# Two layers of linear attention and MLP on one core: one tile transposed before it is scaled, one chunk divided by token, and the queues in a new order

## The chip, the cores and the metric

The kernel runs on one core of a Trainium2 chip. A core has five engines that run their own instruction queues: TensorE (PE in the profile; its weight loads are PEld), VectorE (DVE), ScalarE (ACT), GpSimd (POOL) and SyncE (SP, which here only issues DMAs). They wait for each other with semaphores. The metric is the device time of one execution in microseconds, lower is better.

## The reference

The input is x with 2048 tokens of 512 features. Two layers follow; each is attention and then an MLP, with the same weights in both layers.

```python
def _layernorm(x, axis=-1, eps=1e-5):
    m = jnp.mean(x, axis=axis, keepdims=True)
    v = jnp.var(x, axis=axis, keepdims=True)
    return (x - m) / jnp.sqrt(v + eps)

def _A_ref(x, wqkv, wo):            # 32 heads of 16
    q, k, v = qkv[0], qkv[1], qkv[2]
    phi = lambda t: jnp.where(t > 0, t + 1, jnp.exp(t)) + 1e-6
    pq, pk = phi(q), phi(k)
    kv = jnp.einsum("bhsd,bhse->bhde", pk, v)
    z = jnp.einsum("bhsd->bhd", pk)
    num = jnp.einsum("bhqd,bhde->bhqe", pq, kv)
    den = jnp.einsum("bhqd,bhd->bhq", pq, z)[..., None] + 1e-6
    o = num / den
    ...
def _B_ref(x, w1, b1, w2, b2):
    y = _layernorm(x, axis=-1)
    h = _gelu(jnp.einsum("bsd,df->bsf", y, w1) + b1)
    return jnp.einsum("bsf,fd->bsd", h, w2) + b2

x = x + _A_ref(_layernorm(x, axis=-1), A_wqkv, A_wo)
x = x + _B_ref(_layernorm(x, axis=-1), B_w1, B_b1, B_w2, B_b2)
... # and both lines once more
```

Since kv and z are sums over all tokens, no token's attention output can be formed before every key of the layer is known.

## The kernel before

**Tiles.** The 2048 tokens are 16 tiles of 128 rows, in four chunks of four tiles. The code counts layers, chunks and tiles from zero; an operation's name holds the layer, the tile (or the chunk and a number in it), and sometimes a part: `K0_3` is the key projection of tile 3 in layer 0, `Q0_1_2` the query projection of part 2 of chunk 1, `W10_0_13_1` the up projection of layer 0, chunk 0, column block 13, second half of the chunk. The titles' "layer one" is layer 0 in the code, the "second chunk" is chunk 1, and "tile one" is tile 0.

**One layer.** For each tile: `stats` and `aggr` (DVE, lines 773 and 775) give mean and variance, `veps` (DVE or POOL, 780) adds epsilon, `pow` (POOL, 782) gives the reciprocal root, and `norm` writes the normalised tile y in bf16 (DVE 795, or ACT 790 with POOL's `nmr`). Tile 3 of layer 0 has its sums made by ACT (`sum`, `neg`, `sq`, lines 764 to 770). y is transposed, either by PE through an identity into PSUM (`PTA`, 817) and copied out by ACT (`tc`, 827), or by a DMA transpose that SP issues (`TA`, 804). In layer 0 tiles 0 to 5 go by PE, the other ten by DMA. Then come `K` (four matmuls, 866) and `phi` (834 to 856: ACT `exp` and mostly ACT `relu`, DVE `min`, and a sum on DVE or POOL), and `G`, which sums y transposed times phi(k) over all tiles (958 in layer 0), `Z` (941), which sums phi(k), and `Q` (883 by token, 896 by feature) with its own phi.

**The end of an attention block.** `KV` (1008) times the values' weights, masked per head, and `M` (1031) times the output weights fold all of the keys and values into one 512 x 512 matrix. `WO` (1097) multiplies a tile of phi(q), divided by its denominator, by that matrix; `RA` (DVE, 1102) adds the residual and sets the bank of PSUM free.

**The denominator** (`attn_den`, 1035 on) has two forms, and the table `WAY` says which chunk takes which. By feature: per chunk four `D` matmuls (1074) against a masked z, ACT `ln` (1076) and `rec` (exp of minus it, 1078), and a product `pr` (1082). By token: `pz` (a product of phi(q) with z's row, 1051, POOL or DVE), `red` (a sum per head, DVE, 1054), `den` (adds 1e-6, 1057), `rec` (DVE, 1059), `pr` (1063, POOL or DVE), and then `TP`, a DMA transpose that SP issues (1067). z's row is `zrow`, which PE's `ZR` (1022) and ACT's `cpz0` (971) make. Before, chunks 0 and 1 of layer 0 and chunk 0 of layer 1 go by feature, the others by token.

**The MLP.** A second normalisation (`statsB`, `powB`, `normB`, `TB`), the up projection `W1` (1127), ACT's gelu (1132), the down projection `W2` (1163) and `RB`. `b2` (1113) adds the bias to the residual. In the last layer `OD` stores each tile. The last tile of all, 15, is computed in two halves of columns, h0 and h1, with an addition (1155) and a store (1157) of its own for each.

**The order.** Each engine's queue is written out in `CONF["ORDER"]`, a list of names for each of the five. `CONF["PLACES"]` says which operation uses which buffer and bank after which other, and `CONF["WAY"]` which engine does an operation that more than one can do. A program works out the semaphore waits from this. An engine never passes an operation that waits.

**The start.** PE first runs `warm0` and `warm1`, together fifteen matmuls of 512 columns on constants (747), and then `PTA0_0`, `PTA0_1`, `K0_0`. The loads of x, of the key weights `wk` and the query weights `wq` are issued by SP and ACT; the bias loads `b1` and `b2` by SP among the transposes (`b2` between `TA0_12` and `TA0_10`), `Tb1` transposes b1, and ACT's `b1c` copies it. The weights `wv`, `wo`, `w1`, `w2` are loaded by POOL, after all of layer 0's transposes.

## Time and profile before

| what | us |
|---|---|
| median of three runs | 328.95 (328.55 to 329.53) |
| the profiled execution | 327.5 |
| its span, first to last instruction | 326.3 |
| ACT busy, POOL busy in it | 193.1, 152.5 |
| busy time of DVE, and its share of the span | 211.0, 65% |
| the last matmul group starts at | 322.44 |

The span is the time from the first to the last instruction of one execution that was recorded by the profiler. Busy times are for each engine alone, and the engines work side by side, so they do not add up to the span. A line that is 1% of the span is 3.3 us. The duration of a matmul in the records includes its way through the array: groups of matmuls follow each other sooner than their durations say, and the chain of waits shows the times from start to start.

In the tables, "<-" in a group's name stands between what an instruction writes and what it reads; "idle before" is the time in which the engine stood still ahead of that group, with the name of what it waited for.

### The profile page before, as it was taken

The page shows a single profiled execution, that of the slowest core. Times are in us where ns is not written, and L with a number is a line of the kernel's source. Part 1 is how long each engine was busy: PE and PEld are TensorE (multiplying, and loading weights), DVE is VectorE, ACT ScalarE, POOL GpSimd, SP SyncE. Part 2 cuts the span into 40 slices and gives each one's busy share as a digit, 9 for nine tenths or more (in the row PEclk, how much of TensorE's full clock was granted, in tenths as well). Part 3 has the DMA queues.
Part 4 walks back from the last instruction along what each step waited for, and adds up shares of the span by engine and source line. Part 5 has one row for each costly group of instructions (what it writes and reads, how often), then busy time and mean ns, then how long its engine had stood idle before and what let it go on. Part 6 is the DMA issues. An engine that isn't in the chain of part 4 may idle for free.

```text
span 326.3 us, 4763 instructions
## 1 busy us (share of the span) xinstructions
PE 322.2 (99%) x1723; PEld 159.3 (49%) x1723; DVE 211.0 (65%) x503; ACT 193.1 (59%) x334; POOL 152.5 (47%) x224
## 2 busy tenths in 40 slices
PE   8999999999999999999999999999999999999997
PEld 3444445576454444444444444458644444444444
DVE  5987679996938685142436899999989983300112
ACT  4988769797661416529673477969833454551600
POOL 5662548588663417300757434783856593100000
PEclk9999999999999999999999999999999999999999
DMA  7355753334012210331011110012034322200102
GB/s 266 120 83 97 219 189 104 105 64 68 16 32 50 54 26 3 80 64 34 0 32 33 34 32 0 19 32 50 17 82 94 69 48 66 64 0 2 64 0 80
DMA packets 46883, 20.37 MB, mean 62 GB/s; under 512 B 41932, under 2 KB 45388, under 8 KB 46860
## 3 DMA queue, kind: packets, MB, share of 16 engines
q1 hardware_dynamic: 44572, 13.00, 18.8%
q0 software_dynamic: 1056, 4.72, 4.5%
q10 hardware_dynamic: 1232, 2.36, 2.0%
q8 instruction: 13, 0.21, 0.3%
q14 instruction: 10, 0.08, 0.1%
HBM read 8.00 MB, written 2.10 MB: 31 GB/s over the span
## 4 chain that ended last, share of the span: by engine, by line
PE 97%; DVE 1%; ACT 1%; issue 0%
PE ps L1127 30%; PE ps L1163 29%; PE ps L1097 9%; PE ps L866 8%; PE ps L883 5%; PE ps L987 4%; PE ps L958 4%; PE ps L896 2%; PE ps L747 2%; PE ps L1150 1%; PE ps L1074 1%; PE ps L1008 1%; PE ps L1031 1%; PE ps L941 1%; PE ps L817 0%; DVE pkb L854 0%
## 5 line engine op out<-in xcount | busy, mean ns | idle before, releaser
L1132 ACT ACTIVATE gT<-ps,b1c 128x512 bf16<-128x512 f32 (+1 forms) x140 | 77.1, 600 | 65.3 <-PE ps L1127 65.0
L1127 PE MATMUL ps<-t,w 128*128 128x512 bf16 (+1 forms) x560 | 102.2, 336 | 0.0
L1163 PE MATMUL ps<-w,gT 128*128 128x512 bf16 x434 | 97.6, 379 | 0.0
L1127 PEld LDWEIGHTS ps<-t,w 128*128 128x128 bf16 x560 | 54.6, 98 | 43.7 <-ACT t L827 0.3
L1163 PEld LDWEIGHTS ps<-w,gT 128*128 128x128 bf16 x434 | 42.5, 98 | 50.4 <-DVE xsb L1169 0.2
L782 POOL TENSOR_TENSOR rstd<-veps,neghalf 128x1 f32<-128x1 f32 x64 | 37.9, 602 | 33.5 <-DVE veps L780 31.4
L837 ACT ACTIVATE eb<-ps 128x512 bf16<-128x512 f32 x64 | 37.4, 614 | 18.3 <-PE ps L866 10.5
L1173 DVE TENSOR_TENSOR outb<-ps,xsb 128x512 bf16<-128x512 f32 x15 | 10.1, 686 | 46.3 <-PE ps L1163 40.3
L773 DVE BATCH_NORM_STATS2 stats<-xsb 128x6 f32<-128x512 f32 x48 | 32.3, 678 | 0.4
L848 ACT ACTIVATE rb<-ps 128x512 bf16<-128x512 f32 x45 | 26.6, 617 | 9.2 <-PE ps L866 8.7
L866 PE MATMUL ps<-wqkv,t 128*128 128x512 bf16 x128 | 31.6, 379 | 0.1
L1097 PE MATMUL ps<-gtb,t 128*128 128x512 bf16 x128 | 31.2, 379 | 0.1
L850 DVE TENSOR_SCALAR eb<-eb 128x512 bf16<-128x512 bf16 x45 | 14.0, 321 | 21.1 <-ACT eb L837 21.1
L1113 POOL TENSOR_TENSOR xsb<-xsb,b2b 128x512 f32<-128x512 f32 x20 | 24.3, 1224 | 6.8 <-ACT yb L790 6.6
L790 ACT ACTIVATE yb<-xsb,nmr,rstd 128x512 bf16<-128x512 f32 x21 | 16.7, 812 | 14.2 <-POOL nmr L787 13.9
L780 POOL TENSOR_SCALAR veps<-mv 128x1 f32<-128x1 f32 x35 | 7.6, 217 | 30.8 <-DVE mv L775 28.1
L1063 POOL TENSOR_TENSOR t<-t,rr 128x512 bf16<-128x512 bf16 x14 | 15.5, 1114 | 13.6 <-DVE rr L1059 12.9
L795 DVE TENSOR_SCALAR yb<-xsb,mv,rstd 128x512 bf16<-128x512 f32 x27 | 16.1, 602 | 8.5 <-POOL rstd L782 8.3
L1051 POOL TENSOR_TENSOR lr<-t,zrow 128x512 f32<-128x512 bf16 x15 | 17.9, 1191 | 5.7 <-ACT zrow L971 4.2
L883 PE MATMUL ps<-wqkv,t 128*128 128x512 bf16 x80 | 19.9, 379 | 0.0
L1097 PEld LDWEIGHTS ps<-gtb,t 128*128 128x128 bf16 x128 | 12.3, 98 | 14.7 <-DVE rr L1059 0.6
L866 PEld LDWEIGHTS ps<-wqkv,t 128*128 128x128 bf16 x128 | 12.0, 98 | 14.9 <-ACT t L827 1.0
(97 smaller groups left out, 373.5 us busy)
## 6 DMA issues: line engine op xcount, KB each, us to landing
w<-in_B_w_dram POOLq DMA_DIRECT2D x4, 896.0 KB, 6.9
out_dram<-outb SPq DMA_DIRECT2D x15, 128.0 KB, 1.9
t<-in_A_x_dram ACTq DMA_DIRECT2D x3, 512.0 KB, 4.6
t<-yb SPq DMA_TRANSPOSE x56, 2.5
wqkv<-in_A_wqkv_dram ACTq DMA_DIRECT2D x1, 512.0 KB, 5.8
wqkv<-in_A_wqkv_dram POOLq DMA_DIRECT2D x1, 512.0 KB, 4.6
wo<-in_A_wo_dram POOLq DMA_DIRECT2D x1, 512.0 KB, 5.5
t<-in_A_x_dram SPq DMA_DIRECT2D x1, 384.0 KB, 3.1
```

The costliest lines, as they stand in the source:

```text
L773: G.op("dve", lambda e: e.bn_stats(stats[:, s.slot, :], src()), 620, reads=src_keys, writes=[k + "s"], tiles=[s, *src_tiles], name=f"stats ...
L782: G.op("pool", lambda e: e.tensor_tensor(rstd[:, s.slot:s.slot + 1], veps[:, s.slot:s.slot + 1], neghalf[:], op=ALU.pow), 570, reads=[k + ...
L837: G.op("act", lambda e: e.activation(eb[:, et.slot, :], bank(bt), ACT.Exp), 478, reads=[src_key], writes=[f"e{tag}"], tiles=[bt, et], name ...
L848: G.op("act", lambda e: e.activation(rb[:, rt.slot, :], bank(bt), ACT.Relu), 478, reads=[src_key], writes=[f"r{tag}"], tiles=[bt, rt], nam ...
L866: ins = e.matmul(bank(b), lhsT=yTa(yT)[:, dt, k * P:(k + 1) * P], rhs=wqkv[:, dt, D:2 * D], start=(dt == 0), stop=(dt == DT - 1))
L883: ins = e.matmul(bank(b), lhsT=yTa(yT)[:, dt, k * P:(k + 1) * P], rhs=wqkv[:, dt, 0:D], start=(dt == 0), stop=(dt == DT - 1))
L1051: lambda e, r=r, tok=tok: e.tensor_tensor(lr[:, r.slot, :], tok(), zrow[:], op=ALU.mult), 1150 if on_pool else 600,
L1097: ins = e.matmul(bank(wb), lhsT=yTa(pq)[:, kt, k * P:(k + 1) * P], rhs=gtb[:, kt, :], start=(kt == 0), stop=(kt == DT - 1))
L1113: G.op("pool" if on_pool else "dve", lambda e: e.tensor_tensor(xsb[:, st, :], xsb[:, st, :], b2b[:], op=ALU.add), 1120 if on_pool else 600 ...
L1127: ins = e.matmul(bank(b, n), lhsT=w1[:, dt, ft * P:(ft + 1) * P], rhs=yTa(yT)[:, dt, k0 * P:k1 * P], start=(dt == 0), stop=(dt == DT - 1))
L1132: G.op("act", lambda e, ft=ft, b=b, k0=k0, k1=k1, n=n: e.activation(gT[:, g.slot, ft * 512 + k0 * P:ft * 512 + k1 * P], bank(b, n), ACT.Ge ...
L1163: ins = e.matmul(bank(b), lhsT=gT[:, g.slot, ft * 512 + k * P:ft * 512 + (k + 1) * P], rhs=w2[:, ft, :], start=(ft == 0), stop=(ft == FT - 1))
```

## The change

The change has six parts.

1. **Tile 0 of layer 0 is only centred for the key path.** A new DVE operation `cenA0_0` subtracts the mean as soon as `aggr` has it. PE transposes this centred tile (`PTC0`), ACT copies it (`tcC0`), and `K0_0` multiplies it. The factor 1/std, which is one number for each token and so for each row of K's result, goes into the `scale` of `expk0_0` and `reluk0_0`. The normalised tile is still made, for `G0_0` and `Q0_0`, and reaches its transposed form by a DMA (`TA0_0`).
2. **Tiles 4 and 5** are transposed by DMA and no longer by PE.
3. **Chunk 1 of layer 0 is divided by token**: its `D`, `ln` and `rec` of ACT go, and `pz`, `red`, `den`, `rec` (DVE) and `TP` come.
4. **`b1`, `b2` and the two masks' constants** are created after the loop over tiles; both loads now wait for all sixteen transposes.
5. **The warm-up** is 7 matmuls of 512 columns and 8 of 256, with `PTC0` among them. The last tile is cut at column 384 and no longer at 256, and its narrow part comes first.
6. **All five orders, the buffers, and the engine of many small operations** are arranged anew. Among these: on DVE come b20_7, 10, 12, 13, 15 and b21_6, 10, 11, 14, and to POOL go b20_1, 2 and b21_7, 8, 15; the sums `za` 1, 4, 6, 7, 8, 9, 11 move from POOL to DVE; `pz` and `pr` of chunks 1 to 3 are dealt out differently.

```diff
-    WARM=[[512, 512, 512, 512, 512, 512, 512, 512, 512, 512, 512], [512, 512, 512, 512]],
+    WARM=[[512, 512, 512, 512, 512, 512, 512], [256], [256], [256], [256], [256], [256], [256], [256]],
...
-            "warm0 warm1 PTA0_0 PTA0_1 K0_0 PTA0_2 K0_1 PTA0_3 K0_2 PTA0_4 G0_0_0 K0_3 K0_4 Q0_0_0 G0_1_0 PTA0_5 Q0_0_1 K0_5 "
+            "warm0 warm7 warm6 warm5 PTC0 warm4 warm3 warm2 warm8 warm1 K0_0 PTA0_2 PTA0_1 K0_2 PTA0_3 K0_1 G0_0_0 K0_3 "
+            "Q0_0_2 Q0_0_0 K0_4 Q0_0_1 G0_1_0 G0_2_0 K0_5 G0_3_0 K0_7 Z0_0 G0_4_0 K0_13 Q0_1_3 K0_6 Q0_1_0 G0_5_0 Q0_1_2 "
...
-        def norm(src, src_keys, src_tiles, double, on_act, tag, src16=False, head=False):
+        def norm(src, src_keys, src_tiles, double, on_act, tag, src16=False, head=False, centred=None):
...
+            mean = lambda: stats[:, s.slot, 2:3] if by_act else mv[:, s.slot, 0:1]
+            if centred is not None:
+                yc = Tile(YB, f"yc{tag}")
+                G.op("dve", lambda e: e.tensor_scalar(yb[:, yc.slot, :], src(), mean(), None, op0=ALU.add if by_act else ALU.subtract),
+                     300, reads=[k + "m", *src_keys], writes=[f"yc{tag}"], tiles=[s, yc, *src_tiles], name=f"cen{tag}", lat=40, fast=True)
+                centred.append((yc, f"yc{tag}", s, k + "r"))
...
-        def phi(bt, src_key, dst, dst_key, dst_tiles, tag):
+        def phi(bt, src_key, dst, dst_key, dst_tiles, tag, scaled=None):
...
-            G.op("act", lambda e: e.activation(eb[:, et.slot, :], bank(bt), ACT.Exp), 478, reads=[src_key], writes=[f"e{tag}"],
-                 tiles=[bt, et], name=f"exp{tag}", lat=90, table="exp")
+            by = (lambda: 1.0) if scaled is None else (lambda: rstd[:, scaled[0].slot:scaled[0].slot + 1])
+            more_tiles, more_keys = ([], []) if scaled is None else ([scaled[0]], [scaled[1]])
+            G.op("act", lambda e: e.activation(eb[:, et.slot, :], bank(bt), ACT.Exp, scale=by()), 478, reads=[src_key, *more_keys],
+                 writes=[f"e{tag}"], tiles=[bt, et, *more_tiles], name=f"exp{tag}", lat=90, table="exp")
...
-                for h in range(2):
+                for h, (c0, c1) in enumerate(((0, 3 * P), (3 * P, D))):
...
-                if eng(f"TA0_{st}") == "pe":
+                cen = [] if eng(f"cen{st}") else None
+                y, ykey = norm(lambda c=c, k=k: x0ap(c, k), [("x0", st)], [x0[c]], False, False, f"A0_{st}", src16=True,
+                               head=eng(f"stat{st}"), centred=cen)
+                if cen:
+                    yTc = yTc or Tile(T4, f"yTc{c}")
+                    yc, yckey, sc, sckey = cen[0]
+                    transpose_pe(yc, yckey, yTc, k, f"yTc{st}", f"C{st}", True)
+                    tr = transpose(y, ykey, yT, k, f"yT0_{st}", f"A0_{st}")
+                elif eng(f"TA0_{st}") == "pe":
...
-                if st == 0:
-                    dma("sp", lambda e: e.dma_start(b1r[0:FT, :], B_b1.rearrange("(ft p) -> ft p", p=P)), ["b1r"], name="b1", kb=4,
-                        after=[tr])
...
-                pk = attn_k(0, c, k, yT)
+                pk = attn_k(0, c, k, yTc, f"yTc{st}", (sc, sckey)) if cen else attn_k(0, c, k, yT)
...
+        dma("sp", lambda e: e.dma_start(b1r[0:FT, :], B_b1.rearrange("(ft p) -> ft p", p=P)), ["b1r"], name="b1", kb=4, after=trs)
+        dma("sp", lambda e: e.dma_start(b2b[:], bass.AP(B_b2.tensor, B_b2.offset, [[0, P], [1, D]])), ["b2b"], name="b2", kb=128, after=trs)
+        consts()
```

The parts of the new orders that the prediction walks through, per queue (`D0_1`, `PTA0_4` and `PTA0_5` are gone from PE's):

```text
SP    x0 x1 wk0 TA0_0 TA0_4 TA0_5 TA0_7 TA0_13 TA0_6 TA0_12 TA0_15 TA0_14 TA0_9 TA0_8 TA0_11 TA0_10 b1 Tb1 b2 TP0_1_1 TP0_1_3 TP0_1_0 TP0_1_2 TB0_0 TB0_1
ACT   wk1 xc1 sumA0_3 tcC0 xc3 sqA0_3 wq tcA0_2 expk0_0 tcA0_1 reluk0_0 expk0_2 tcA0_3 expk0_1 xc2 reluk0_1
DVE   ones statsA0_0 aggrA0_0 cenA0_0 statsA0_2 aggrA0_2 statsA0_1 aggrA0_1 vepsA0_1 normA0_2 normA0_0 normA0_1 statsA0_4 normA0_3
DVE   dz0 pr0_0_2 pz0_1_3 red0_1_3 den0_1_3 cpg0_1 cpg0_2 cpg0_0 cpg0_3 red0_1_0 kvm0_1 kvm0_3 kvm0_2 red0_1_1 kvm0_0 den0_1_1 den0_1_0
      rec0_1_1 minq0_2_0 cpm0_2 rec0_1_3 pr0_0_1 red0_1_2 rec0_1_0 den0_1_2 phiq0_2_0 rec0_1_2 RA0_0 statsB0_0 RA0_1
POOL  phik0_14 wv wo w1_0 phik0_8 phiq0_1_1 w1_1 w2_0 w2_1 pr0_0_0 pz0_1_0 pr0_0_3 pz0_1_1 pz0_1_2 pr0_1_1 pr0_1_3 pr0_1_0 pr0_1_2 vepsB0_0 powB0_0
PE    K0_9 K0_8 K0_11 K0_10 G0_7_0 Q0_1_1 Q0_0_3 Z0_3 G0_8_0 Z0_2 G0_9_0 G0_10_0 D0_0_2 D0_0_3 D0_0_0 G0_11_0 ZR0
PE    WO0_0_0 WO0_0_1 WO0_0_2 WO0_0_3 WO0_1_0 WO0_2_0 Q0_2_3 WO0_5_0 WO0_3_0 Q0_3_2 WO0_7_0 WO0_6_0 WO0_4_0 W10_0_4_0
PE    W21_9_7 W21_10_7 W21_15_h1 W21_15_h0
```

## The prediction

> **What bounds the kernel now.** I read the page first, for who is busy and when.
>
> ```profile
> span 326.3 us, 4763 instructions
> PE 322.2 (99%) x1723; PEld 159.3 (49%) x1723; DVE 211.0 (65%) x503; ACT 193.1 (59%) x334; POOL 152.5 (47%) x224
> ...
> PE   8999999999999999999999999999999999999997
> ```
>
> PE (TensorE) sets the time: only the first and last of 40 slices are not full. So a change pays by taking work off PE, by starting PE's real work sooner, or by closing a gap. The view of waits, for PE alone, has every gap (total, times, longest):
>
> ```profile
> PE ps L747 <- PEq L1315: 0.8, 1, 0.8
> PE ps L941 <- DVE pkb L854: 0.7, 1, 0.7
> PE ps L817 <- DVE yb L795: 0.2, 1, 0.2
> ```
>
> Then the start, in the timeline (start, duration, engine, line):
>
> ```profile
> 0.84 6.34 PE L747 MATMUL ps<-const-bfloat16-1.0 128*128 128x512 bf16 x15 [0.84 <-PEq L1315]
> 4.99 0.41 DVE L795 TENSOR_SCALAR yb<-t,mv,rstd 128x512 bf16<-128x512 bf16 x1 [0.68 <-POOL rstd L782]
> 7.01 0.39 PE L817 MATMUL ps<-idp,yb 128*128 128x128 bf16 x4
> 8.09 1.04 PE L866 MATMUL ps<-wqkv,t 128*128 128x512 bf16 x4
> 12.26 1.03 PE L866 MATMUL ps<-wqkv,t 128*128 128x512 bf16 x4
> ```
>
> The fifteen warm-up matmuls of 512 columns take 6.34 us, 0.42 each; real ones of that size later take 0.216 (a group of four 0.86 in the chain of waits). So the array runs at half rate until about 7.0, although the page's clock row shows 9 throughout. K0_0 begins at 8.09, K0_3 at 12.43 by the chain. Last, busy time by stage, and prices (a by-form list: count, total, mean ns, idle before):
>
> ```profile
> 12.40:33.50 21.10, 21.10 (x130) 9.79 (x128) 17.46 (x56) 18.68 (x34) 11.05 (x26) 1.00 0.42 70
> 40.00:72.00 32.00, 32.00 (x203) 17.78 (x201) 28.76 (x68) 27.23 (x52) 19.89 (x24) 1.00 0.41 123
> L1051 POOL TENSOR_TENSOR lr<-t,zrow 128x512 f32<-128x512 bf16 x15 | 17.9, 1191 | 5.7 <-ACT zrow L971 4.2 <-DVE t L854 1.0 <-DVE t L843 0.2
> L1063 POOL TENSOR_TENSOR t<-t,rr 128x512 bf16<-128x512 bf16 x14 | 15.5, 1114 | 13.6 <-DVE rr L1059 12.9 <-DVE mv L775 0.7
> L1054 DVE TENSOR_REDUCE rd<-lr 128x32 f32<-128x512 f32 x20 | 13.5, 675 | 3.7 <-POOL lr L1051 3.6
> ```
>
> The columns of the windows are PE, PEld, DVE, ACT, POOL. From 40 to 72 DVE has 3.2 us idle in 32 beside a full PE: this is where the change adds DVE work.
>
> **The start.** Before, tile 0 needs stats, aggr, veps, pow and normalise (done 5.40), then waits for the warm-up (7.18). After, cenA0_0 follows aggr (ends 4.12) at once: 4.16 plus a normalise of 0.41 gives 4.57. The cut warm-up (7 of 512, then 3 of 256, at 0.42 per 512) ends at 4.4, so PTC0 runs at about 4.6 (4 transposes, 0.43 at half rate) and five warm-ups of 256 last to 6.1. ACT does sumA0_3 (4.42 to 5.15), then tcC0 (0.60) to 5.8. K0_0 begins near 6.1 at half rate, and if the rate doubles at 7.0 as before it ends at 7.5.
>
> From there ACT paces it (0.60 an instruction, 0.52 to 0.55 start to start). On DVE, statsA0_2, aggr, statsA0_1, aggr, veps, normA0_2, normA0_0, normA0_1 (0.6 to 0.69, 0.18, 0.15, 0.41) end at 6.95, 7.4 and 7.8. PTA0_2 at 7.5, tcA0_2 7.85, expk0_0, tcA0_1, reluk0_0 to 10.0; K0_2 at 8.4, K0_1 at 9.3, phik0_0 at 10.45, G0_0 to 11.35. So K0_3 starts at 11.35 against 12.43: 1.08 us sooner, of which PTA0_4, now a DMA transpose, is 0.22. What cen adds to DVE (0.41) is in this walk; loads xc3, wq, xc2 are issued later on ACT, but wq (5.8 us to land, issued about 6.9) is wanted at 12.2.
>
> **PE work removed.** PTA0_4 (counted) and PTA0_5: 0.22 each. The four D0_1 matmuls: 4 x 0.216 = 0.87. Splitting the last tile 384 + 128 instead of 256 + 256 changes nothing on PE: columns are equal, and pairs of weight load and 128-column matmul already run at 0.055 (a transpose group of four takes 0.22).
>
> **The gap at 39.8.** PE waits 0.66 for the last phik of Z0_2. After, Z0_2 follows K0_10 by four groups and Z0_3 (3.9 us), while expk, min and three phi need 2.1; the gap goes. Bounds 0 to 0.66; I take 0.66.
>
> **DMA.** TA0_0, TA0_4 and TA0_5 join SP's queue of ten (1.25 to issue, 2.5 to land). TA0_0 goes out at 7.4, lands 9.9, wanted by Q0_0_2 at 12.2; TA0_4 at 11.0, lands 13.5, wanted at 13.95; TA0_5 at 14.1, 16.6, wanted at 17.4. Priced at nothing; the cover is thin for TA0_4. b2 no longer stands before TA0_10; b1, Tb1 and b2 wait for all sixteen tiles, with only TP0_1 behind them on SP until the 50s. b1c stands earlier on ACT (about 45); b1's load and Tb1 (4.7 to land) give about 40. On POOL the late weight loads now precede pr0_0_0, two fewer (0.97 each) among the products.
>
> **Chunk one divided by token.** ACT loses four ln (0.70) and four rec (0.64). DVE gains four red (0.68), four den (0.19), four rec (0.34) and one pz (0.74) = 5.6 us; POOL gains three pz (1.19) and four pr (1.11), less two old products; SP four transposes (2.4 to land). Walking it: cpz0 comes at 42.7. POOL runs six pr and three pz, waiting on DVE's rec for the last four, until 55.0. DVE reaches RA0_0 at 53.9 (54.52 before), with red0_1_2, rec and phiq0_2_0 queued ahead. PE reaches WO0_0 at 52.5 (53.40 before), with two more Q groups (1.73) behind it: a lead of 2.6. From here RA paces it, because WO0 cycles through three banks: WO0_6 waits for RA0_3 (59.8), 0.4 lost. vepsB0_0, pow, normB0_0, RA0_2, normB0_1 put TB0_1 out at 58.8, landing 61.3, as PE gets there at 61.5 (63.98 before). TB0_3 lands near 71.3, wanted by W10_0_12_1 at 72.1.
>
> **The rest.** Veps, b2 and zacc move between POOL and DVE; from 64 to 190 DVE is busy 77 of 126 us, so 12 more fit. From 190 to 256 it is 60.9 of 66, and I count 2.7 added (two za, net one pz and one b2, less three veps). I charge nothing; bounds -0.13 (the gap at 250 closes) and +0.66 (one wait as long as the longest here).
>
> **The tail.** h0 now ends it with 384 columns: DVE between 0.42 (256) and 0.69 (512), 0.55, so +0.13; its DMA between 1.7 (64 KB) and 1.9 (128 KB): +0.1. Together +0.2.
>
> **Sum.** Start 0.86, PTs 0.44, D 0.87, gap 0.66 = 2.83 gained; 0.4 and 0.2 given back: 2.2. The profiled execution took 327.5 (span 326.3 and 1.2 around it): 325.3. The runs' median is 328.95, 1.45 above it; I take the same 2.2 off: 326.7.
>
> **The clock.** In this trace half rate lasts some 6.2 us from the first matmul (0.84 to about 7.0), and the sum above uses that. The Trainium skill (TensorE: Matmul & The Clock Gate, Part 1) says that one free-running window of 3.4 us must be busy throughout, which as an estimate from its figure puts the change of rate 3.4 to 6.8 us after the start; the 6.2 lie inside. Part 4 of the page says that transposes do not count as busy in the same way: this speaks against PTC0 in the midst of the warm-up, and is rival one. At the early end of that rule K0_0 would run at full rate and the sum gain 0.85 more.
>
> **Rivals.**
> 1. The rate doubles late. If PE's activity counts anew from PTC0 (4.6), the same 6.2 us end at 10.8. K0_0, two transposes, K0_2, PTA0_3 and K0_1 at half rate put K0_3 at 12.5 instead of 11.35: 1.15 lost, 327.8. For it: less continuous warm-up. Against: PE idles only some 0.2 us in it.
> 2. Early DMA transposes land late. The slowest took 4.3; then TA0_4 lands at 15.3, 1.35 after K0_4 wants it: 328.1. For it: the four loads, all issued by 7.44 before, kept the DMA share near 1.0 to 11, and now run later. Against: nine of ten in this stage took about 2.5.
> 3. Slower: DVE bounds the stretch from cpz0 to normB0_3. Its 28.8 us of 40 to 72 grow by 5.6, less 0.7 (two pr leave, one comes) and 0.3 (veps): 4.6. If its 3.2 idle there stay (they are waits for ACT and POOL), normB0_3, 68.7 before, ends at 72.4 with the start's 0.86 taken off; TB0_3 lands 2.5 later, 74.9, where PE wanted it at 72.1: 2.8 lost, 329.5; with POOL's nine products at their slowest (1.58 and 1.51 instead of 1.19 and 1.11) the waits grow by up to 3.6, to 333.1. It decides from normB0_3 at 69.6, and loses to before from 71.8. For it: DVE waits behind red for POOL's pz and POOL behind DVE's rec. Against: ACT is relieved and later pz work is moved out of the stretch.
> 4. The new order opens waits in layer two (190 to 256), where DVE has 5.1 idle and gets 2.7: 1.5 lost, 328.2.
>
> **How the numbers follow.** A run cannot be told from no change within 0.3%, 0.99 us: 327.96 to 329.94. Chances: forecast 0.58, rival one 0.08, two 0.08, three 0.16, four 0.10. Rival one at 327.8 lies at the line, half each side. Faster 0.58 + 0.04 = 0.62. Rival three spans the upper line from 329.5 on; I give 0.06 of it to same, 0.10 to slower. Same: 0.04 + 0.08 + 0.10 + 0.06 = 0.28. Slower: 0.10. The likeliest case alone spans 325.3 (no stalls, early clock, gap at 250 closed) to 327.4 (one more wait). The whole range runs 325.2 to 329.2; outside it are rival three and a gain above 3.7, together under 0.2.
>
> **What would show it.** K0_0 near 6.1 and K0_3 near 11.35; no wait on Z's L941 row; D matmuls 8 instead of 12 on their line; WO0_0 near 52.5; the first W10 near 61.5; tail 0.2 longer. Wrong if the first W10 comes after 63, if PE's waits sum to over 2 us, or if PE at half rate lasts past 8.

## The result, and the profile after

The changed kernel takes 326.75 us by the median of three executions (326.62, 326.75, 326.81), the kernel before in the same comparison 328.9 (328.55 to 329.53): 2.15 us less, and a ratio of 0.9932 with an interval of [0.9912, 0.9951]. A fourth execution of the changed kernel took 1928.44 us, with the matmuls about six times slower throughout, which no other execution of any version here did; it stands outside the median and the ratio, and the last section shows it.

The profile after is that of another execution of the unchanged new kernel (e1_again below): 326.49 us, span 325.2. From its page:

```profile
span 325.2 us, 4760 instructions
...
PE 319.3 (98%) x1711; PEld 157.8 (49%) x1711; DVE 220.0 (68%) x534; ACT 195.3 (60%) x330; POOL 138.4 (43%) x210
...
PE   7899999999999999999999999999999999999996
```

PE still sets the time. Its busy time fell by 2.9 us (from 322.2), but the span only by 1.1 (from 326.3): more of the span is now waiting. DVE is busy for 9.0 us more and POOL for 14.1 less, in keeping with the work that moved from POOL to DVE. The view of waits for PE says where the waiting is (total, times, longest):

```profile
PE ps L750 <- PEq L1332: 0.8, 1, 0.8
PE ps L877 <- DMA t<-yb: 0.8, 1, 0.8
PE ps L877 <- DMA wqkv<-in_A_wqkv_dram: 0.8, 1, 0.8
PE ps L952 <- DVE pkb L854: 0.7, 1, 0.7
PE ps L877 <- ACT t L836: 0.2, 1, 0.2
```

The first line is the beginning of the program and was there before. The line of K is 877 now, that of Z 952. Two waits of K are new and large: one for a DMA transpose, one for the load of the key weights. The wait of Z, which the prediction let go, stands as it was. Together the waits are 3.3 us, where they were 1.7 before. The timeline of PE at the start (start, duration, engine, line):

```profile
0.83 3.79 PE L750 MATMUL ps<-const-bfloat16-1.0 128*128 128x512 bf16 x10 [0.83 <-PEq L1332]
4.58 0.61 PE L826 MATMUL ps<-idp,yb 128*128 128x128 bf16 x4
...
6.62 1.02 PE L877 MATMUL ps<-wqkv,t 128*128 128x512 bf16 x4 [0.76 <-DMA wqkv<-in_A_wqkv_dram]
...
11.53 1.03 PE L877 MATMUL ps<-wqkv,t 128*128 128x512 bf16 x4
...
15.05 1.02 PE L877 MATMUL ps<-wqkv,t 128*128 128x512 bf16 x4 [0.77 <-DMA t<-yb]
```

PTC0 is at 4.58, K0_0 at 6.62 (8.09 before), K0_3 at 11.53 (12.26 before, in the same view), and K0_4 stands 0.77 us for its tile. The windows that the prediction showed of before read now (PE, PEld, DVE, ACT, POOL, clock, DMA share, GB/s):

```profile
12.40:33.50 21.10, 20.33 (x123) 9.51 (x122) 18.63 (x61) 18.62 (x34) 11.06 (x26) 1.00 0.44 94
40.00:72.00 32.00, 32.00 (x193) 17.44 (x191) 29.70 (x73) 21.33 (x41) 26.69 (x33) 1.00 0.48 143
```

PE is full from 40 to 72 as before. ACT lost 5.9 us there (27.23 before), POOL gained 6.8 (19.89), DVE 0.9 (28.76).

**Where the gain lies.** The line of W1 tells when the first up projection starts; the rest of the span is everything behind it.

| version | first W1 | span | from there to the end |
|---|---|---|---|
| before, as recorded | 63.8 | 326.3 | 262.5 |
| before, another execution (e5) | 65.0 | 327.5 | 262.5 |
| after (e1) | 62.8 | 325.2 | 262.4 |

All of the gain between these executions is made ahead of the first W1; the first layer's MLP and all of layer two, with their new orders, differ by 0.1 us. In the ten other profiles below the last column is between 262.0 and 263.0.

### The profile page after: what moved, and what is told of

Its sections match the earlier page's. It is cut to its first block, busy times and chain, and to the rows that moved or that the text cites. A ratio compares the mean times of both kernels' runs of the same rounds, so it can differ in the third digit from the quotient of the medians.

```text
span 1927.2 us, 4730 instructions
## 1 busy us (share of the span) xinstructions
PE 1895.8 (98%) x1681; PEld 529.2 (27%) x1711; DVE 219.1 (11%) x534; ACT 201.4 (10%) x330; POOL 135.0 (7%) x210
## 4 chain that ended last, share of the span: by engine, by line
PE 98%; issue 1%; ACT 0%; DVE 0%
PE ps L1138 30%; PE ps L1175 29%; PE ps L877 9%; PE ps L1108 8%; PE ps L894 7%; PE ps L969 4%; PE ps L998 4%; PE ps L907 2%; PE ps L1161 1%; PE ps L750 1%; PE ps L1085 1%; PE ps L1019 1%; PE ps L1042 1%; PE ps L826 0%; PE ps L952 0%
## 5 line engine op out<-in xcount | busy, mean ns | idle before, releaser
L1138 PE MATMUL ps<-t,w 128*128 128x512 bf16 (+1 forms) x553 | 598.7, 1440 | 6.6 <-issue 6.6
L1175 PE MATMUL ps<-w,gT 128*128 128x512 bf16 x426 | 576.6, 1706 | 7.5 <-issue 7.5
L1138 PEld LDWEIGHTS ps<-t,w 128*128 128x128 bf16 x560 | 181.4, 324 | 421.5 <-issue 419.8
L1175 PEld LDWEIGHTS ps<-w,gT 128*128 128x128 bf16 x434 | 140.1, 323 | 426.6 <-issue 425.2
L877 PE MATMUL ps<-wqkv,t 128*128 128x512 bf16 x124 | 173.4, 1708 | 3.7 <-issue 2.8
L1108 PE MATMUL ps<-gtb,t 128*128 128x512 bf16 x123 | 172.2, 1702 | 4.7 <-issue 3.7
L894 PE MATMUL ps<-wqkv,t 128*128 128x512 bf16 x95 | 133.2, 1708 | 0.9 <-issue 0.9
L998 PE MATMUL ps<-pkb,yb 128*128 128x512 bf16 x61 | 85.0, 1700 | 2.8 <-issue 2.8
L969 PE MATMUL ps<-pkb,yb 128*128 128x512 bf16 x62 | 85.8, 1699 | 1.8 <-issue 1.8
L877 PEld LDWEIGHTS ps<-wqkv,t 128*128 128x128 bf16 x128 | 40.7, 320 | 120.6 <-issue 119.3
L894 PEld LDWEIGHTS ps<-wqkv,t 128*128 128x128 bf16 x96 | 31.0, 324 | 92.2 <-issue 91.0
L907 PE MATMUL ps<-t,wqkv 128*128 128x512 bf16 x32 | 44.3, 1702 | 0.0
L998 PEld LDWEIGHTS ps<-pkb,yb 128*128 128x128 bf16 x64 | 20.4, 322 | 60.9 <-issue 60.8
L969 PEld LDWEIGHTS ps<-pkb,yb 128*128 128x128 bf16 x64 | 19.5, 312 | 57.6 <-issue 55.6
```

Source lines behind the costliest of these rows:

```text
L877: ins = e.matmul(bank(b), lhsT=yTa(yT)[:, dt, k * P:(k + 1) * P], rhs=wqkv[:, dt, D:2 * D], start=(dt == 0), stop=(dt == DT - 1))
L894: ins = e.matmul(bank(b), lhsT=yTa(yT)[:, dt, k * P:(k + 1) * P], rhs=wqkv[:, dt, 0:D], start=(dt == 0), stop=(dt == DT - 1))
L907: ins = e.matmul(bank(b), lhsT=wqkv[:, dt, kt * P:(kt + 1) * P], rhs=yTa(yT)[:, dt, :], start=(dt == 0), stop=(dt == DT - 1))
L969: ins = e.matmul(ps[:, gb.slot + dc, :], lhsT=yb[:, y.slot, dc * P:(dc + 1) * P], rhs=pkb[:, pk.slot, :], start=(st == 0), stop=(st == ST ...
L998: ins = e.matmul(bank(b), lhsT=yb[:, ys[k].slot, dc * P:(dc + 1) * P], rhs=pkb[:, pks[k].slot, :], start=(k == 0), stop=(k == 3))
L1108: ins = e.matmul(bank(wb), lhsT=yTa(pq)[:, kt, k * P:(k + 1) * P], rhs=gtb[:, kt, :], start=(kt == 0), stop=(kt == DT - 1))
```

## The experiments

All twelve kernels compute the full result. They ran in three batches of four, e1 to e4, e5 to e8 and e9 to e12; the kernel before took 328.66 (327.53 to 331.02), 329.23 (327.25 to 330.64) and 329.21 (327.25 to 331.12) in them. A time is the median, with the lowest and the highest; a ratio is to the kernel before of the same batch, with its 95% interval. Where the orders were written anew the line numbers are some 190 higher: K is then line 1064, 1071, 1072 or (e10) 1039, the transposes by PE 1013, 1020, 1021 or (e10) 990.

### e1: the change once more

No edit.

> The changed kernel once more, for an undisturbed profile and a tighter time. My theory (start, removed PE work and the closed gap add up to 2.2 us): ratio to before 0.991 to 0.995; K0_0 near 6.1 us, K0_3 near 11.35, no wait of PE at Z, WO0_0 near 52.5, the first W10 near 61.5, the tail 0.2 longer. Rival (the gain comes from elsewhere, layer two's new order for example): the first W10 after 62.8 and the rest of the 2.2 us behind it.

Measured: 326.77 (326.16 to 327.93, seven executions), ratio 0.9933 [0.9905, 0.9962], as expected. Its profile is the one above: of the theory's signs K0_0, K0_3, the wait of Z and WO0_0 did not come as said, and the first W10 came near the rival's 62.8 and not at 61.5. But no more of the gain lies behind it, so the rival fails too.

### e5: the kernel before once more

No edit; a single execution.

> The kernel before, once more, for the scatter of its executions (327.5 to 331.0 so far, while its recorded profile was of 327.5). Theory one (the moment at which PE's rate doubles moves from run to run): K0_0's four matmuls or the warm-up differ, and K0_3 moves with them by 0.5 to 1.5 us; everything behind it has the same spacing. Theory two (late transposes or a stage further on): K0_3 stays at 12.3 to 12.4 and a wait elsewhere on PE carries the difference.

Measured: 328.8, span 327.5. Two rows of PE's waits matter, and one piece of its chain of waits (start, duration, what):

```profile
PE ps L866 <- DMA t<-yb: 1.2, 1, 1.2
...
PE ps L941 <- DVE pkb L854: 0.7, 1, 0.7
```

```profile
16.90 4.10 DMA t<-yb
```

The execution that the prediction was made on had no wait for a DMA transpose. This one, 1.3 us longer and much nearer to the median, has one of 1.2: TA0_6, issued at 16.90, landed 4.1 us later and K0_6 stood. In the recorded execution the same transpose took 2.6. That fits theory two: K0_3 begins at 12.21 here and at 12.26 there, although the fifteen warm-up matmuls took 5.96 us and not 6.34, so the moment at which the rate doubles did move and K0_3 did not follow it. The recorded execution was a quick one: of the 52 executions of the kernel before in the three batches only two took less than its 327.5. Between these two profiles one transpose that landed in time makes the difference. How many executions carry such a wait two profiles cannot tell.

### e2: the last tile cut in the middle, as before

```diff
-                for h, (c0, c1) in enumerate(((0, 3 * P), (3 * P, D))):
+                for h, (c0, c1) in enumerate(((0, 2 * P), (2 * P, D))):
```

> The changed kernel with the last tile cut into 256 and 256 columns again, in the changed order (h1 first, h0 last). My theory: the tail is 0.2 us shorter, 0.13 of it in the last addition (0.42 instead of 0.55) and the rest in the last store. Rival (a store's fixed time hides its size): 0.1 or less.

Measured: 325.99 (325.83 to 326.25), ratio 0.9904 [0.9876, 0.9932]. The last addition of DVE, first in e1, then in e2:

```profile
322.75 0.56 DVE L1167 TENSOR_TENSOR outb<-ps,xsb 128x384 bf16<-128x384 f32 x1
```

```profile
322.48 0.42 DVE L1167 TENSOR_TENSOR outb<-ps,xsb 128x256 bf16<-128x256 f32 x1
```

The addition is 0.14 shorter, and the last store takes 1.77 from issue to the end of the span (322.93 to 324.7) and not 1.87 (323.33 to 325.2): 0.24 together. The uneven cut costs that much. The medians differ by 0.78, more than the tail gives. The two profiles differ by 0.5: besides the tail the first W1 is 0.27 sooner in e2, because K0_0 begins at 6.21 there and at 6.62 in e1, with no edit at that place; in e1 it waits for the load of the key weights. The other 0.3 of the medians no profile shows.

### e4 and e8: tile 0 normalised ahead of its transpose

In e4 `cenA0_0` is gone, PTA0_0 takes the place of PTC0, and the short warm-up stays around it. In e8 all eight warm-ups of 256 columns run ahead of PTA0_0.

```diff
-DVE   aggrA0_0 cenA0_0 statsA0_2 ... normA0_2 normA0_0 normA0_1
+DVE   aggrA0_0 normA0_0 statsA0_2 ... normA0_2 normA0_1
-PE    warm0 warm7 warm6 warm5 PTC0 warm4 warm3 warm2 warm8 warm1 K0_0
+PE    warm0 warm7 warm6 warm5 PTA0_0 warm4 warm3 warm2 warm8 warm1 K0_0       (e4)
+PE    warm0 warm7 warm6 warm5 warm4 warm3 warm2 warm8 warm1 PTA0_0 K0_0       (e8)
-SP    x0 x1 wk0 TA0_0 TA0_4
+SP    x0 x1 wk0 TA0_4
```

> The changed kernel with tile 0 normalised before its PE transpose (no cenA0_0, no TA0_0, no scale in expk0_0), the short warm-up kept. Theory one (the centred path brings the early start): K0_0 0.6 us later at 6.7, the normalisations of tiles 2 and 1 0.1 to 0.5 later, 0.3 to 0.5 us slower in all. Theory two (the shorter warm-up alone brings it, since K0_0 runs at half rate before 7.0 anyway): within 0.15 us of the changed kernel.

> No centring, as before in this study, but all eight 256-column warm-ups stand ahead of PTA0_0, so that PE is busy until y0 is there (5.5). In the first kernel without centring PE stood still for 0.96 before PTA0_0 and ran at half rate until 8.7 instead of 5 to 7. Theory one (that idle time held the rate down, and centring is worth only a late K0_0): at least 0.6 us of its 1.1 us loss comes back, and the rate doubles before 7.7. Theory two (the later first tile itself costs the 1.1): within 0.3 us of the first kernel without centring.

Measured: e4 327.85 (325.9 to 328.21), ratio 0.9953 [0.9928, 0.9978]; e8 325.89 (325.73 to 327.53), ratio 0.9917 [0.9893, 0.994]. PE's timeline, e4 first:

```profile
5.58 0.61 PE L1020 MATMUL ps<-idp,yb 128*128 128x128 bf16 x4 [0.96 <-DVE yb L998]
...
7.04 1.91 PE L1071 MATMUL ps<-wqkv,t 128*128 128x512 bf16 x4
```

```profile
5.62 0.40 PE L1020 MATMUL ps<-idp,yb 128*128 128x128 bf16 x4 [0.44 <-DVE yb L998]
...
6.83 1.02 PE L1071 MATMUL ps<-wqkv,t 128*128 128x512 bf16 x4 [0.81 <-DMA wqkv<-in_A_wqkv_dram]
```

In e4 PE stood 0.96 us for the normalised tile in the midst of the warm-up, and K0_0's four matmuls, 7.04 to 8.75, still ran at half rate (1.91 for the group, against 1.02). In e8 PTA0_0 is as late (5.62), but PE was busy until 5.18, and the four transposes already run at full rate (0.40, against 0.61). By the medians e4 is 1.1 slower than e1, more than either of its theories said, and e8 has all of that back. So most of e4's loss is the hole in the warm-up, and centring is not the whole of the early start. How much of it is centring is read best at G0_0, the first group behind the keys of tiles 0 to 2, before first, then e1 and e8:

```profile
11.40 1.03 PE L958 MATMUL ps<-pkb,yb 128*128 128x512 bf16 x4
```

```profile
10.65 1.04 PE L969 MATMUL ps<-pkb,yb 128*128 128x512 bf16 x4
```

```profile
10.88 1.03 PE L1163 MATMUL ps<-pkb,yb 128*128 128x512 bf16 x4
```

In the six profiles with centring (e1, e2, e3, e6, e7, e9) G0_0 begins at 10.14 to 10.65, in the three without it but with the full warm-up ahead of PTA0_0 (e8, e11, e12) at 10.84 to 10.88. So some 0.5 of the gain at this place comes without centring (0.22 of it because PTA0_4 no longer stands ahead), and centring adds 0.2 to 0.7. That e8's median is nevertheless the lower one has another reason in its profile: it has no wait of Z0_2 (e9 below), which costs e1 0.7.

### e10: the short warm-up alone, in the kernel before

```diff
-    WARM=[[512, 512, 512, 512, 512, 512, 512, 512, 512, 512, 512], [512, 512, 512, 512]],
+    WARM=[[512, 512, 512, 512, 512, 512, 512], [256, 256, 256, 256, 256, 256, 256, 256]],
```

> The kernel before with its warm-up alone cut to the changed kernel's length (7 of 512, then 8 of 256, all ahead of PTA0_0). Theory one (from the run without centring that began PE's real work at 5.6: the long warm-up, not the normalised tile, held the start back): K0_0 near 6.7 instead of 8.1, K0_3 near 11.5 instead of 12.4, 0.6 to 1.1 us faster than before. Theory two (DVE and ACT pace the first 12 us whenever PE starts): within 0.3 us of before.

Measured: 329.0 (327.71 to 330.31), ratio 0.9992 [0.9967, 1.0017]: nothing. PE's timeline, and below it a window (PE, PEld, DVE, ACT, POOL, then the granted clock, DMA share and GB/s):

```profile
5.48 0.40 PE L990 MATMUL ps<-idp,yb 128*128 128x128 bf16 x4 [0.17 <-DVE yb L968]
7.60 0.40 PE L990 MATMUL ps<-idp,yb 128*128 128x128 bf16 x4 [1.72 <-DVE yb L968]
7.83 1.56 PE L1039 MATMUL ps<-wqkv,t 128*128 128x512 bf16 x4
...
10.04 1.80 PE L1039 MATMUL ps<-wqkv,t 128*128 128x512 bf16 x4
```

```profile
8.10:11.50 3.40, 3.15 (x12) 1.21 (x11) 3.10 (x8) 2.21 (x4) 1.67 (x5) 0.51 0.86 325
```

The full rate was there at 5.48 (0.40 for four transposes). Then PTA0_1, which in this order stands ahead of K0_0, waited 1.72 us for its tile, and from 8.1 to 11.5 the granted clock is 0.51: the half rate came back for 3.4 us and took away what the shorter warm-up had won. K0_3 begins at 13.85 here, later than the 12.26 of before. Not every execution shows this: six of the twelve have a mean clock of 0.995 like this one, with a median of 330.06, and the other six a clock of 1.00 and 328.66, some 0.5 under the kernel before. In the new order K0_0 stands ahead of PTA0_1, so that its start does not hang on tile 1; no run changes that alone.

The Trainium skill (TensorE: Matmul & The Clock Gate, Part 1) has a free-running window of about 3.4 us after which the rate changes, and puts the fall to half rate behind at least one idle window. The 3.4 us at 0.51 agree with the length of the window. The second half is not what this run shows: 1.72 us of idling came before the fall, half of a window.

### e9: one sum of phi from POOL to DVE

The gap of Z0_2 did not close, and the timelines of DVE and of POOL in e1 (in this order) show what lies ahead of it:

```profile
34.92 1.39 DVE L861 TENSOR_SCALAR eb<-eb 128x512 bf16<-128x512 bf16 x1 [0.68 <-ACT eb L848]
36.23 1.30 DVE L852 TENSOR_SCALAR eb<-eb 128x512 bf16<-128x512 bf16 x1
```

```profile
35.45 0.73 POOL L729 DMA_DIRECT2D w<-in_B_w_dram  x1
36.20 1.16 POOL L865 TENSOR_TENSOR pkb<-eb,rb 128x512 bf16<-128x512 bf16 x1
```

Two DVE operations on the way to Z0_2, which take 0.29 elsewhere, took 1.39 and 1.30, and each ended within 0.2 us of the end of a POOL instruction: the first at 36.31 (the DMA issue of 35.45 ends at 36.18), the second at 37.53 (POOL's `phik0_8`, 36.20 on, ends at 37.36). The same pair was there before, in the recorded execution, POOL's timeline first and DVE's second:

```profile
36.55 1.17 POOL L854 TENSOR_TENSOR pkb<-eb,rb 128x512 bf16<-128x512 bf16 x1
```

```profile
36.76 1.25 DVE L854 TENSOR_TENSOR pkb<-eb,rb 128x512 bf16<-128x512 bf16 x1
```

DVE's sum takes 0.42 when POOL is quiet and 1.25 here. So `phik0_8` was moved to DVE.

```diff
-POOL  phik0_14 wv wo w1_0 phik0_8 phiq0_1_1
+POOL  phik0_14 wv wo w1_0 phiq0_1_1
-DVE   mink0_8 mink0_11 mink0_10
+DVE   mink0_8 mink0_11 phik0_8 mink0_10
```

> The changed kernel with phik0_8 on DVE (behind mink0_11) and no longer on POOL. In the changed kernel PE still waited 0.7 for Z0_2, and two DVE operations before it that usually take 0.3 took 1.39 and 1.30, each ending as a POOL instruction ended (a DMA issue, then phik0_8). Theory one (POOL's work stretches DVE's short bf16 operations): the second of them falls to 0.3, the wait at Z goes or halves, 0.3 to 0.6 us faster than the changed kernel. Theory two (ACT's exp is late, DVE only follows): the wait stays, within 0.2 us.

Measured: 325.74 (325.39 to 326.4), ratio 0.99 [0.9866, 0.9934]. Its waits of PE, all of them, and DVE's two operations:

```profile
PE ps L1072 <- ACT yb L994: 0.9, 1, 0.9
PE ps L945 <- PEq L1527: 0.8, 1, 0.8
PE ps L1021 <- DVE yb L999: 0.2, 1, 0.2
```

```profile
34.75 0.29 DVE L1056 TENSOR_SCALAR eb<-eb 128x512 bf16<-128x512 bf16 x1 [0.68 <-ACT eb L1043]
...
35.50 0.29 DVE L1047 TENSOR_SCALAR eb<-eb 128x512 bf16<-128x512 bf16 x1
```

Both take 0.29 and the wait of Z is gone. The median is 1.0 under e1's; the intervals of the two ratios overlap, so the missing wait is the better evidence. (The 0.9 in the first row is K0_4 again. The profile names ACT, but TA0_4 landed at 14.74 and K0_4 began at 14.88.)

The other profiles bear it out, with one exception. With `phik0_8` on POOL the pair takes 1.38 to 1.51 and 1.30 in e1, e2, e3, e4, e6 and e7, and Z waits 0.7 to 0.8 in each. With it on DVE, in e9, e11 and e12, both take about 0.3 and Z does not wait. The exception is e8: `phik0_8` is on POOL, but the pair took 0.30 and 0.94, and Z did not wait. So it seems that the sum on POOL makes the wait only where the two operations fall badly against POOL's queue.

The Trainium skill (SBUF — State Buffer, Who interferes with whom) says that DVE and GpSimd share a pair of ports to SBUF under an exclusive lock, and that a DVE instruction in its two-port modes or with two inputs from SBUF stands still until the other is through. The second stretched operation and the one of before agree: they end 0.17 us (37.53 against 37.36) and 0.3 us after POOL's. The first does not follow from it alone: it ran beside DMA issues of POOL, and in e9 POOL issues the same two DMAs beside the same two operations, and neither is stretched. Its cause stays open.

### e6: tile 4 transposed by PE again

```diff
-SP    x0 x1 wk0 TA0_0 TA0_4 TA0_5
+SP    x0 x1 wk0 TA0_0 TA0_5
-PE    K0_1 G0_0_0 K0_3
+PE    K0_1 G0_0_0 PTA0_4 K0_3
-ACT   expk0_1 xc2
+ACT   expk0_1 tcA0_4 xc2
```

> The changed kernel with tile 4 alone transposed by PE again (PTA0_4 behind G0_0, tcA0_4 behind expk0_1). The changed kernel's K0_4 waited 0.76 for TA0_4, which took 3.96 to land instead of 2.5. Theory one (rival two of the prediction: early DMA transposes land late among the loads): PE's wait for the transpose goes, 0.22 of PE work and an ACT copy come, 0.3 to 0.6 us faster than the changed kernel. Theory two (ACT paces this stretch anyway): within 0.2 us.

Measured: 326.56 (325.17 to 327.45), ratio 0.9927 [0.9903, 0.9952]; 0.2 less than e1 by the medians, which is inside the scatter. The wait of K0_4 is gone, but another took its place:

```profile
PE ps L1102 <- ACT rb L1054: 1.3, 1, 1.3
```

Q0_0_2 stood for tile 0's own transpose, TA0_0, which went out at 7.25 and landed at 13.50, 6.3 us later (the profile names ACT). The time from issue to landing of the DMA transposes of layer 0, read one by one, has a pattern:

```text
issued at:landed after    first            second           third            fourth
before, recorded          15.35: 2.6       16.98: 2.6       18.45: 2.5       19.88: 3.6
e5                        15.20: 2.6       16.90: 4.1       18.82: 2.7       20.49: 2.4
e1                         7.59: 4.5       10.95: 4.0       13.38: 2.5       15.21: 2.4
e2                         7.42: 4.4       10.61: 4.0       13.04: 2.4       14.86: 2.4
e3                         7.60: 4.0       10.79: 4.5       13.22: 2.5       15.04: 2.4
e9                         7.36: 4.7       10.55: 4.2       12.98: 2.4       14.80: 2.4
e7                         7.25: 4.6       10.85: 4.6       13.29: 2.5       15.11: 2.4
e6                         7.25: 6.3       12.87: 2.9       14.71: 2.4       18.67: 3.2
e8                        11.15: 4.2       13.58: 2.5       15.40: 2.4       18.86: 3.3
e4                        12.30: 4.1       14.73: 2.4       16.55: 2.4       19.92: 3.2
e12                       11.12: 4.3       13.55: 2.5       15.37: 2.4       18.95: 3.5
e11                       13.54: 3.0       15.40: 2.5       17.88: 4.5       19.12: 4.0
```

In the nine profiles of the new order that have one, every transpose issued before 12.4 took 4.0 us or more; those issued from 12.8 to 15.4, in all twelve profiles of the list, took 2.4 to 3.0. The windows give a reason, before first and then e1 (the last but one number is the DMA share):

```profile
10.00:12.00 2.00, 2.00 (x16) 1.13 (x15) 1.99 (x8) 2.00 (x5) 0.04 (x1) 1.00 0.47 190
12.00:14.00 2.00, 2.00 (x10) 0.80 (x9) 2.00 (x7) 2.00 (x6) 1.70 (x5) 1.00 0.00 0
```

```profile
10.00:12.00 2.00, 2.00 (x11) 0.74 (x9) 1.83 (x5) 2.00 (x5) 0.74 (x2) 1.00 0.82 122
12.00:14.00 2.00, 2.00 (x11) 0.84 (x9) 2.00 (x9) 1.50 (x4) 0.94 (x2) 1.00 1.03 287
```

Before, the loads of x and of the query weights are done by 12 and the first transpose goes out at 15.35. After, the last load of x is issued at 10.72, lands 3.6 us later, and the two early transposes run beside such loads. The landing times are closer still (us; the load named is the last one issued ahead of the transpose):

```text
      query weights landed, then TA0_0      last load of x landed, then the next transpose
e1    11.53   12.08                         14.36   14.91 (TA0_4)
e2    11.24   11.77                         14.08   14.64 (TA0_4)
e6    12.88   13.50                         15.21   15.78 (TA0_5)
e4    -       -                             15.89   16.43 (TA0_4)
```

In all nine profiles these transposes landed 0.5 to 0.6 us behind the load that was issued ahead of them, which points to the load as what sets the time. The slow execution of the last section gives a check: there no load was issued between 3.21 and 13.36, and TA0_0, out at 7.21, took 2.5. The lateness of TA0_4 is therefore no accident of one execution. Whether an earlier last load of x would cure it no run shows. The transposes near 17 to 19 that now and then take 4 us have no load beside them, and their cause stays open.

### e3 and e7: chunk 1 divided by feature again

All of chunk 1's `pz`, `red`, `den`, `rec` by token, `pr` behind them and `TP` go, and `D`, `ln`, `rec` and `pr` by feature come back. e7 is e3 with the `ln` and `rec` of parts 2 and 3 further back on ACT and `WO0_3` ahead of `WO0_5` on PE.

```diff
-        "den0_1": "tok",
-SP    TP0_1_1 TP0_1_3 TP0_1_0 TP0_1_2
+PE    G0_13_0 D0_1_1 G0_14_0 D0_1_0 ... Q0_3_0 D0_1_2 ... WO0_0_3 D0_1_3
+ACT   ... rec0_0_3 ln0_1_1 rec0_1_1 ln0_1_0 rec0_1_0 ...
+ACT   cpm0_0 ln0_1_2 rec0_1_2 expq0_2_1 ln0_1_3 rec0_1_3        (e3)
+ACT   expq0_2_1 reluq0_2_1 ln0_1_2 rec0_1_2 ln0_1_3 rec0_1_3    (e7)
```

> The changed kernel with chunk 1 of layer 0 divided by feature again: D, ln and rec back, pz, red, den and TP gone, placed by hand. My theory (four D matmuls are PE work on the path): 0.87 us slower than the changed kernel, less up to 0.4 that PE no longer waits for RA0_3. Rival (DVE and POOL bound the stretch before W10, so that dividing by token costs what it saves): within 0.3 us of the changed kernel, or faster.

> Chunk 1 divided by feature again, with ln0_1_2 and ln0_1_3 behind reluq0_2_1 on ACT and WO0_3 ahead of WO0_5, so that no WO0 of chunk 0 waits for them (in the first such kernel one WO waited 2.6). My theory (four D matmuls are path work): 0.5 to 1.2 us slower than the changed kernel. Rival (the token form costs on DVE and POOL what it saves on PE, since the first W10 began at 62.9 and not at 61.5): within 0.3 us of it or faster.

Measured: e3 332.53 (331.08 to 333.55), ratio 1.0096 [1.006, 1.0132]; e7 329.34 (327.91 to 330.52), ratio 1.0002 [0.9981, 1.0024]. One wait of e3 spoils it:

```profile
PE ps L1295 <- ACT rb L1046: 2.6, 1, 2.6
```

A WO waited for a bank whose `reluq0_2_1` stood behind the new `ln` on ACT. The wait cost more than itself. It ended at 59.32, and the window behind it reads (the clock is the last but two):

```profile
59.41:62.82 3.41, 3.41 (x9) 1.23 (x10) 1.59 (x5) 0.00 (x0) 1.27 (x3) 0.50 0.00 0
```

For these 3.4 us PE ran at half rate: eight matmuls of WO took 3.55 us, where eight take 1.89 a little later. Four of e3's six executions have the same mean clock of 0.995. All this was the placing, not the form, so e3 says nothing of the form. In e7 that wait is gone, and of PE's waits these are new or larger than in e1:

```profile
PE ps L1064 <- DMA t<-yb: 1.6, 2, 1.4
...
PE ps L1295 <- DVE xsb L1300: 0.6, 2, 0.4
...
PE ps L1272 <- ACT lr L1274: 0.2, 1, 0.2
```

Against e1 the ratio is 0.0069 higher, 2.3 us. Of that the four matmuls are 0.87 and the waits for RA and `ln` 0.8; the transposes' 0.8 more is of the kind seen under e6. Another placing of this form may do better than this one, so 1.7 (0.87 and 0.8) is what the token form gained against it, and only the 0.87 does not hang on the placing. Neither the theory's 0.5 to 1.2 nor the rival's 0.3 held.

### e11 and e12: what the runs point to, together

e11 has e8's start, e6's tile 4, e9's `phik0_8` and e2's tail; e12 is the same with tile 4 by DMA.

> The changed kernel without centring and with the full warm-up ahead of PTA0_0, tile 4 by PE, phik0_8 on DVE and the last tile cut in the middle. If the parts add up: the version without centring had 325.9, less 1.0 for K0_4's wait plus 0.2 of PE work, less 0.2 in the tail, less up to 0.3: 324.6 to 325.0, ratio to before 0.986 to 0.990. If another early transpose is late instead (TA0_5), or ACT paces: 325.5 or more.

> The same with tile 4 by DMA as in the changed kernel: the difference to the one before is tile 4 alone. Theory one (the early transpose lands late): 0.5 to 0.9 us slower than the one before, with a wait at K0_4. Theory two: within 0.2 us.

Measured: e11 325.69 (325.05 to 326.84), ratio 0.9899 [0.9865, 0.9933]; e12 325.84 (325.53 to 327.14), ratio 0.9908 [0.9874, 0.9942]. Both are quicker than before and, by the medians, than the change. But the sum that was expected, 324.6 to 325.0, did not come: four edits together give no more than `phik0_8` alone (325.74), and tile 4 by PE no more than 0.15 by the medians (0.6 between the two profiles). One reason is that e11 and e12 are without centring: their G0_0 begins at 10.84 and 10.85, e9's at 10.25. The other is the waits of PE for a transpose, 0.5 in e11 and 1.1 in e12:

```profile
PE ps L1071 <- DMA t<-yb: 0.5, 1, 0.5
```

```profile
PE ps L1071 <- DMA t<-yb: 1.1, 1, 1.1
```

In e11 a later transpose, issued at 17.88, took 4.5 us, and its wait is half of the one that tile 4 had removed.

## Why the prediction was right, and where it was not

The forecast for the median, 326.7, came out (326.75, and 326.77 in e1), and faster was right. The sum behind it was not right: between the profiled executions it forecast 2.2 us, and they differ by 1.0. That the median was met is luck, as the end of this section shows. Of the prediction's three signs of being wrong one came, PE's waits of over 2 us (3.3), and the first W10 at 62.92 missed another by 0.08.

| step | predicted | measured in e1 |
|---|---|---|
| K0_0 starts | 6.1 | 6.62 |
| K0_3 starts, gain against before in the same view | 1.08 | 0.73 |
| TA0_4, wait of K0_4 | 0 | 0.77 |
| D matmuls in all | 8 | 8 |
| wait of Z0_2 | 0 (0.66 gained) | 0.7 |
| WO0_0 starts | 52.5 | 54.27 |
| WO0_6 waits for RA | 0.4 | 0 |
| first W10, by the chain of waits | 61.5 | 62.92 |
| the tail | +0.2 | +0.24 |

**The start** came, but 0.35 smaller: K0_3 was to begin 1.08 sooner and began 0.73 sooner (12.26 and 11.53 both in the timeline; the prediction's 12.43 for before is the chain's number, which stands 0.17 later). The rate did not double at 7.0 as before: K0_0's four matmuls at 6.62 took 1.02, the full rate, which is the case of an earlier clock that the prediction set beside the sum. What bound K0_0 was not the clock but its weights, issued at 1.70 and landed at 6.53 by the chain of waits; before, K0_0 at 8.09 hid that load, and the prediction has no term for it. The two errors met: K0_0 began 0.5 late and ran 0.5 faster, and PTA0_2 followed it at 7.48 where the walk has 7.5. (By that walk full rate saves K0_0 some 0.5, not the 0.85 that the prediction gives it.) So the 0.35 was lost behind K0_0. Where the weights land sooner K0_0 begins at 6.15 (e9) or 6.21 (e2), as predicted. Centring was credited with bringing the start; by e8, e11 and e12 it brings 0.2 to 0.7 at G0_0, and some 0.5 come without it.

**"The gap goes, I take 0.66" failed.** Its reason was that four groups and Z0_3 lie between K0_10 and Z0_2, 3.9 us, while the exp, min and phi need 2.1. The durations used for these were those of DVE alone. Beside POOL's DMA issues and its sum two of them took 1.39 and 1.30 instead of 0.29, 2.1 more than counted, where the room was 1.8. The gap of before had the same neighbour. e9 takes it away.

**"TA0_4 priced at nothing" failed.** The prediction called its cover thin (wanted at 13.95, landing 13.5) and made the late landing rival two, with 0.08. The rival's mechanism came true: 4.0 us and not 2.5, a wait of 0.77 where the rival had 1.35. The evidence named for it, loads that run later than before, is what the landing times under e6 show. The evidence against it was misread: of the ten transposes of this stage before, eight took about 2.5 and two 3.6 and 4.1. It deserved more than 0.08, since in every profile of this order a transpose out before 12.4 is late.

**Chunk one by token**: the D matmuls are 0.87 less, as said. In the view of lines by form:

```profile
L1085 PE MATMUL ps<-t,zb x8: 379/379/390, 41.8 to 203.8; 128*128 128x512 bf16 x8
```

WO0_0 came 1.77 later than predicted; TA0_4, the gap and K0_3 are 1.82 (0.77, 0.7 and 0.35). From WO0_0 to the first W10 the prediction had 9.0 with the wait of WO0_6 for RA0_3 in it; by the chain it was 8.65 (54.27 to 62.92), and no wait of WO is in the list. So the 0.4 given back was not given back, and rival three (DVE bounds this stretch) did not come. It had DVE's busy time from 40 to 72 grow by 4.6, and it grew by 0.9: the added `red`, `rec`, `den` and `pz` are there, but the new order also takes phi work, a b2 and a `pr` off DVE in this stretch, some 5 us where the prediction counted 1.0. Against the one other placing that was tried, e7, the form gains more than the matmuls, up to 1.7.

**The tail** is right: 0.24. **Layer two** was charged nothing, and 262.4 against 262.5 agrees; with the tail's 0.24 inside, what lies between the first W1 and the tail gains some 0.3, and rival four did not come. **Rival one**, the late doubling, did not come either: transposes in the midst of the warm-up did no harm. A late or lost full rate exists all the same. In e4 0.96 us of idling inside the warm-up put it off, and in e10 and e3 idling of 1.72 and 2.57 us took it away again; e1's waits are 0.77 at most, and waits of 1.2 to 1.4 us (e5, e6, e7) show no such loss.

**Why the total fits all the same.** The terms that failed cost 1.8 (0.77 for TA0_4, 0.66 for the gap, 0.35 in the start); the wait of WO0_6 that did not come gave 0.4 back, and the stretch behind the first W1 0.3. Of the 2.2 that leaves 1.1, and like for like the profiled executions differ by 1.0 (327.5 and 326.49). The medians differ by 2.15 (1.9 in e1's batch) because the profiled execution of before was a quick one: the prediction took its 1.45 under the median as a constant and carried it over to the kernel after, whose profiled execution stands 0.28 under its median. e5 shows that most of the 1.45 can be one late transpose (1.2) which K0_6 waited for. Two errors of opposite sign and nearly equal size met, and that is luck. That the 1.2 is a part of most executions of before rests on e5 alone and was not counted, so what the other half of the medians' gain consists of is argued and not shown.

## What to carry to other kernels

Read how far the profiled execution stands from the median, and find the wait that makes the difference before a sum is made against either; a change can remove a wait that the one execution does not show. A slack worked out from an engine's durations holds only for the neighbours that it had: here a short DVE operation beside POOL work, and a DMA transpose issued behind a late load, took several times or nearly twice as long. In these runs a shorter warm-up paid where PE stayed busy behind it, so look at what stands first behind it in the queue.

## What was not expected of the hardware

- **A stretched operation.** DVE operations of 0.29 us took up to 1.39 beside POOL (e1), which was enough to hold the matmuls for 0.7.
- **A transpose behind a load.** A DMA transpose that takes 2.5 us alone landed 0.5 to 0.6 us behind the load issued ahead of it, up to 6.3 us after its own issue (e6).
- **The rate falls back quickly.** 1.72 us of idling in the start were followed by 3.4 us at a granted clock of 0.51 (e10), 2.57 us behind the first WO groups by 3.4 us at 0.50 (e3). The mean clock says that six of e10's twelve executions and four of e3's six had such a stretch.
- **One execution at a sixth of the rate.** Its page:

```profile
span 1927.2 us, 4730 instructions
...
PE 1895.8 (98%) x1681; PEld 529.2 (27%) x1711; DVE 219.1 (11%) x534; ACT 201.4 (10%) x330; POOL 135.0 (7%) x210
```

DVE, ACT and POOL have the busy times of any execution, and PE alone was slow from the first matmul to the last: the first four groups of K take 1.32 us for each matmul of 512 columns from start to start, where e1 has 0.216. The granted clock of that execution is given as 1.00. It was seen once, and nothing here says why.
